# Unequal key halves for four maxima steps of a head pair, and a division that is split between its two multiplications

## The chip, the cores and the metric

The kernel runs on one core of one Trainium2 chip. Its time is the device time of one execution in microseconds, from the first to the last instruction with what lies around them. The engines are TensorE (PE in the profile; PEld is its unit that loads weights), VectorE (DVE), ScalarE (ACT), GpSimd (POOL) and SyncE (SP), which issues most of the DMA transfers.

## The reference

Two blocks follow each other. The first is attention in which a query sees only the keys of its own cluster; the second is a feed-forward block with the activation h * erf(softplus(h)).

```
q, k, v: (4, 8, 768, 64) float32; centroids: (8, 16, 64)
q_assign = argmax(q_n . c_n); k_assign = argmax(k_n . c_n)      # normalised, 16 clusters
mask = q_assign[..., :, None] == k_assign[..., None, :]
scores = where(mask, q @ k^T / sqrt(64), -1e9)
scores = scores - max(scores, axis=-1, keepdims=True)
attn = exp(scores);  attn = attn / (sum(attn) + 1e-9)
x = (attn @ v) as (3072, 512)
h = x @ w_in;  g = h * erf(softplus(h));  out = g @ w_out       # w_in (512, 2048), w_out (2048, 512)
```

## The kernel before, in words

The attention block takes the 32 heads in 16 pairs (p = 0 to 15); the heads of a pair, e = 0 and 1, lie on partitions 0 to 63 and 64 to 127, so the two heads' multiplications use different rows of TensorE's array and run side by side. Each pair has 12 units u: two halves of 384 queries (half), and for each six blocks of 128 keys (j). A period (function `period(p, i)`, i = 0 to 5) works on two units. Everything from the period on is written in the order in which the engines shall do it: the class `InOrder` keeps the program's order on TensorE, VectorE, ScalarE and GpSimd. DMAs on SP are outside of that order there.

**Maxima.** The shift of the softmax of pair p + 1 is made while pair p is worked on. `maxima_step(p, i)` takes 128 queries (block t) against one half of the 768 keys: a product of the queries' and keys' bf16 copies ("qv", "kv"; in the profile wide<-kv,qv), then the cluster mask as a product of one-hot rows ("qm", "km"; wide<-km,qm), both into the PSUM tile `wide`, of which there is one; then VectorE reduces the two heads' rows to their negated maxima, `nmx` (nmx<-wide). Each period does two such steps, the two key halves of one query block: `step_ahead(u)` at its beginning, whole, and `step_ahead(u + 1, True)`, whose three pieces are set between other work. That second step's mask product uses 32 rows of each head, and the scores' mask product the other 32. Because the tile is single, each step's first multiplication waits for the step before to be reduced. The steps of the coming pair begin in period i = 3 of the pair before it: periods 3 and 4 (the fourth and fifth of a pair) have its blocks t = 0 and 1, period 5 has t = 2.

**Units.** `products(u)` multiplies queries and keys in float32 (sc<-qT,kT, two passes each) into one of two PSUM buffers `sc`; `scores(u)` adds the mask and the shift (sc<-qm,km); `curve(u)` is the exponential on ScalarE; `accumulate` sums on GpSimd, and `attend` multiplies by v (turned<-pr,in_v), two units later. A period's order on TensorE is: first maxima step, products of both units, second step's product, scores of the first unit, second step's mask product, scores of the second unit, then (in i = 3 the similarities of pair p + 2 with the centroids) attend, and in i = 0 and 3 the sums for a division.

**Routing.** In i = 3, `choose(p + 2, ...)` finds the clusters on VectorE: a transpose (sims), the maxima of 16 similarities, which it writes into the buffer of the period's second unit (sc<-sims), and the comparison with them (hot<-sims,sc). Between these VectorE does one or two operations on a weight that is being prepared (`bounded`, `shifted`), in pairs 1 to 11.

**Division.** `divide(u)` runs after the last unit of a half, in i = 3 for the first half and in i = 0 for the second. TensorE sums, ScalarE makes the inverse inv, and the generator stops. In the next period it goes on after the first maxima step: VectorE makes `den` and two multiplications in place, one for each k; it stops, and goes on after the second step's maximum with the write of x (more_out<-den,turned) and four DMAs to `x_dram`:

```
        mask(0)()
        next(part[0], None)      # den and the multiplications
        ...
        products(u)
        products(u + 1)
        mask(1)()
        second = step_ahead(u + 1, True) if u > 0 else iter(())
        next(second, None)
        scores(u)
        next(second, None)
        mask(3)()
        next(second, None)       # the second step's maximum
        next(part[0], None)      # x
        scores(u + 1)
```

The feed-forward block that follows uses products of Strassen-Winograd form and isn't touched.

Of the kernel before, what the change touches and what calls it, by code (L numbers as in the profile page):

```python
# [14 lines left out]
ALU = mybir.AluOpType  # L15
ACT = mybir.ActivationFunctionType
AX = mybir.AxisListType
PSUM = bass.MemoryType.PSUM

P = 128  # L20
B, H, S, D = 4, 8, 768, 64
# [4 lines left out]
HW = S // 2  # L26
QW = HW // 2
TW = QW + 2
HJ = NJ // 2
HP = H // 2  # L30
NPAIR = B * HP
# [39 lines left out]
def kernel(  # L71
# [55 lines left out]

    lowest = [const.tile([P, HJ, P], BF16, name=f"lowest{i}") for i in range(2)]
    maxima = [const.tile([P, 2, NJ, 3], F32, name=f"nmx{i}") for i in range(2)]
# [7 lines left out]
    def part_of(i, lo, n):  # L137
        return more_out[:, i].rearrange("p f m -> p (f m)")[:, lo : lo + n]
# [3 lines left out]

    prs = [const.tile([P, 2, 2, TW], F32, name=f"pr{i}") for i in range(NPT)]

# [52 lines left out]
    for base, pattern, sign, op, fill in (  # L197
# [5 lines left out]
            out=first, in_=first, compare_op=op, fill=fill, base=base, pattern=pattern,  # L203
# [61 lines left out]
    for e in range(2):  # L265
        for n in range(2):
            r = e * D + n * Q
# [11 lines left out]
    cn = setup[:, D : 3 * D].rearrange("p (e d) -> p e d", e=2)  # L279
    spare = iter(range(TW, HW))  # L280

# [98 lines left out]
    def maxima_step(p, i, sm=wide, behind=False):  # L380

        st = pairs[p]
        nmx = maxima[p % 2]
        t, half = divmod(i, 2)

        def passes(a, b, start, rows):
            for e in range(2):
                r = slice(e * D + rows.start, e * D + rows.stop)
                te.matmul(
                    sm[:, e, 0:HW], lhsT=st[a][r, t * P : (t + 1) * P],  # L390
                    rhs=st[b][r, half * HW : (half + 1) * HW], start=start, stop=not start,
                )

        passes("qv", "kv", True, slice(0, D))
        if behind:
            yield
        passes("qm", "km", False, slice(Q, D) if behind else slice(0, D))
        if behind:
            yield
        ve.tensor_reduce(  # L400
            out=nmx[:, :, t, half], in_=sm[:, :, 0:HW], axis=AX.X, op=ALU.max, negate=True
        )
        if i in (NJ - 1, 2 * NJ - 1):
            h = i // NJ
            ve.tensor_reduce(
                out=lowest[h][:, :, ::D].rearrange("p t e -> p e t"),
                in_=nmx[:, :, h * HJ : (h + 1) * HJ], axis=AX.X, op=ALU.min,
            )
            turns.append((p, h))

    def turn(p, h, copies=(ae.copy, ae.copy)):

        st = pairs[p]
        pn = turned[h][:, 0:HW].rearrange("p (t n) -> p t n", t=HJ)
        for t in range(HJ):
            for e in range(2):
# [50 lines left out]
    def accumulate(u):  # L467

        p, half, j = units[u]
        st = pairs[p]  # L470
        pr = prs[u % NPT]
        if j == 1:
            st["acc", half] = part_of(1 + half, 0, 2 * HW).rearrange("p (g x) -> p g x", x=QW)
        if j > 0:
            acc = st["acc", half]
            so_far = quarters(prs[(u - 1) % NPT]) if j == 1 else acc
            ge.tensor_tensor(out=acc, in0=so_far, in1=quarters(pr), op=ALU.add)

    def attend(u):

        p, half, j = units[u]
        st = pairs[p]
        if j == 0:
            st["av", half] = turned[half][:, 0 : 2 * TW].rearrange("p (k n) -> p k n", k=2)
        for k in range(2):
            for g in range(4):
                te.matmul(
                    st["av", half][g * Q : (g + 1) * Q, k], lhsT=st["v"][:, j, g // 2, k * Q : (k + 1) * Q],
                    rhs=prs[u % NPT][:, g // 2, g % 2], start=(j == 0 and k == 0), stop=(j == NJ - 1 and k == 1),
                )  # L490

    def divide(u):

        p, half, _ = units[u]
        st = pairs[p]
        av = st["av", half]

        psum = turned[1 - half][:, 0:QW]
        for g in range(4):
            te.matmul(psum[g * Q : (g + 1) * Q], lhsT=minus, rhs=st["acc", half][:, g], start=True, stop=True)  # L500

        if u + 1 < len(units):
            inv = routep.tile([P, QW], F32, name="inv")
            den = routep.tile([P, QW], F32, name="den")
        else:
            inv, den = part_of(0, 4 * HW, QW), part_of(1, 0, QW)
        ae.activation(out=inv, in_=psum, func=ACT.Ln, bias=alleps, scale=-1.0)
        ae.activation(out=inv, in_=inv, func=ACT.Exp, scale=-1.0)
        yield
        ve.scalar_tensor_tensor(  # L510
            out=den, in0=psum, scalar=S * EPS, in1=inv, op0=ALU.subtract, op1=ALU.mult
        )
        for k in range(2):
            raw = av[:, k, 0:QW]
            ve.scalar_tensor_tensor(
                out=raw, in0=raw, scalar=av[:, k, QW : QW + 1], in1=inv, op0=ALU.add, op1=ALU.mult
            )
        yield
        x = part_of(0, (2 * p + half) % 4 * HW, HW).rearrange("p (k x) -> p k x", k=2)
        ve.scalar_tensor_tensor(  # L520
            out=x, in0=den.unsqueeze(1).to_broadcast([P, 2, QW]), scalar=2.0, in1=av[:, :, 0:QW],
            op0=ALU.add, op1=ALU.mult,
        )
        b, r = divmod(p, HP)
        for g in range(4):
            rows_of, at = r * P + g // 2 * D, b * S + half * HW + g % 2 * QW
            nc.sync.dma_start(
                out=x_dram[rows_of : rows_of + D, at : at + QW].rearrange("(k r) x -> r k x", k=2),
                in_=x[g * Q : (g + 1) * Q],
            )  # L530
        if half == 1:
            del pairs[p]
        yield
# [209 lines left out]
    def step_ahead(u, behind=False):  # L743
        p, i = divmod(u + NJ, 2 * NJ)
        steps = maxima_step(p, i, behind=behind) if p < NPAIR else iter(())
        if not behind:
            run(steps)
        return steps
# [7 lines left out]
    def period(p, i):  # L756
# [78 lines left out]
        if u > 0:  # L835
            if i == 1 and early(n1 - 1):
                summed(n1 - 1)
            elif i == 4 and early(n1):
                summed(n1)
            for w in (u - 2, u - 1):  # L840
                accumulate(w)
            if i % HJ == 1 and p in POOL_FORMS and forms:
                forms.pop(0)[1]()
            for w in (u - 2, u - 1):
                attend(w)
            if i % HJ == 0:
                part[0] = divide(u - 1)
                next(part[0])
# [13 lines left out]
    st = pairs[0]  # L862
    st["qT"], st["kT"] = rows[0]["q"], rows[0]["k"]
    ve.transpose(out=st["qT"], in_=st.pop("q").rearrange("p n t -> p (n t)"))
    for e in range(2):
        ve.tensor_copy(
            out=ccT[e * D : (e + 1) * D, :, e * C : (e + 1) * C],
            in_=pct[e * D : (e + 1) * D].rearrange("d (r e c) -> d r e c", e=2, c=C)[:, :, e],
# [7 lines left out]
    for r in (0, D):  # L876
        for half in range(2):
            for e in range(2):
                c = r + half * Q + e * C
                ve.tensor_copy(  # L880
                    out=pick[r : r + D, half, e * D : (e + 1) * D].rearrange("p (n c) -> p n c", n=2)[:, :, 1 : C + 1],
                    in_=first[r : r + D, c : c + C].unsqueeze(1).to_broadcast([D, 2, C]),
# [16 lines left out]
    for i in range(NJ):  # L899
        run(maxima_step(0, i, also if i % 2 else wide))  # L900
        if i == 1:
            masks(0, "q", 1, turned[1])()
        if i < NJ - 1:
            warm(2, turned[0], zeros)
# [20 lines left out]
    for w in (u - 2, u - 1):  # L925
        attend(w)
    last = divide(u - 1)
    attention.close()

# [100 lines left out]
```

## Time and profile before

| | us |
|---|---|
| median of 3 runs | 997.11 (996.61 to 997.18) |
| profiled execution, its own time | 997.0 |
| its span, first to last instruction | 995.3 |
| TensorE busy | 987.6 |
| VectorE busy | 700.5 |
| ScalarE busy | 488.0 |
| GpSimd busy | 350.3 |

Matmuls overlap each other in the array, so "busy" for TensorE says that something was under way, not how well it was used. The granted clock was 1.0 throughout. A line of a timeline gives start and length in us, engine, line (62 for all, since a helper issues them), operation, output<-inputs, shapes and how often; a bracket gives the idle time before it and what is held to have ended it. A line of busy time by stretch gives the stretch and its length, then the busy time of PE, PEld, DVE, ACT and POOL with the number of instructions, the granted clock, the DMA engines' busy share and GB/s. The attention block fills about the first 400 us, 24.6 a pair.

### The profile page before, as it was taken

What the parts mean: (1) busy time and instruction counts of PE and PEld (TensorE: products, weight loads), DVE (VectorE), ACT (ScalarE), POOL (GpSimd) and SP (SyncE); (2) the same over time, 40 slices, a digit from 0 to 9 for tenths busy, and PEclk for the clock granted to TensorE, in tenths of its full rate; (3) what the DMA queues carried; (4) which work ended last, traced back from release to release, by engine and by line L of the source; (5) the groups of instructions that cost most, each with busy time, mean ns of one, the idle gap of its engine ahead of it and who ended that gap; (6) DMA issues with size and microseconds to landing.
All of it is one profiled execution on the core that took longest, in us unless ns stands there. A gap on an engine that the chain in (4) does not pass through costs nothing.

```text
span 995.3 us, 20543 instructions
## 1 busy us (share of the span) xinstructions
PE 987.6 (99%) x8362; PEld 743.0 (75%) x8362; DVE 700.5 (70%) x1347; ACT 488.0 (49%) x659; POOL 350.3 (35%) x237
## 2 busy tenths in 40 slices
PE   8999999999999999999999999999999999999998
PEld 3555555555555555688888888888888888888887
DVE  8888888888888876779676554756475647655653
ACT  3777777777776665575432414150505050505050
POOL 1687878787878888662400000000000000000000
PEclk9999999999999999999999999999999999999999
DMA  9444444444444210331000100010001000000001
GB/s 223 78 110 108 107 110 111 110 113 113 87 94 110 51 35 19 102 106 65 1 12 32 42 1 22 22 43 1 22 22 43 1 21 22 1 1 22 22 1 42
DMA packets 147294, 55.88 MB, mean 56 GB/s; under 512 B 128640, under 2 KB 137088, under 8 KB 147200
## 3 DMA queue, kind: packets, MB, share of 16 engines
q1 hardware_dynamic: 144848, 54.29, 21.5%
q8 instruction: 65, 1.06, 0.4%
q10 hardware_dynamic: 2352, 0.30, 0.2%
q14 instruction: 29, 0.24, 0.1%
HBM read 41.98 MB, written 12.58 MB: 55 GB/s over the span
## 4 chain that ended last, share of the span: by engine, by line
PE 96%; DVE 1%; POOL 1%; DMA 1%; issue 0%; ACT 0%; SPq 0%; ACTq 0%; DVEq 0%; POOLq 0%
PE bank L62 43%; PE turned L62 31%; PE sc L62 16%; PE wide L62 6%; POOL more_out L62 1%; DVE nmx L62 1%; DMA g_more<-in_moe_w_out_dram 0%; DMA in_q<-in_q_dram 0%; DVE sims L62 0%; POOL x_more L62 0%; DVE kT L62 0%; DVE qT L62 0%; ACT pr L62 0%; ACT w_out L62 0%; DVE turned L62 0%
## 5 line engine op out<-in xcount | busy, mean ns | idle before, releaser
L62 POOL TENSOR_TENSOR more_out<-more_out,pr 128x768 f32<-128x768 f32 x128 | 217.0, 1695 | 19.2 <-ACT pr L62 10.5
L62 DVE TENSOR_REDUCE nmx<-wide 128x2 f32<-128x768 f32 x189 | 180.6, 955 | 58.9 <-PE wide L62 57.7
L62 ACT ACTIVATE pr<-sc 128x768 f32<-128x768 f32 x192 | 148.8, 811 | 95.6 <-PE wide L62 91.0
L62 PE MATMUL turned<-pr,in_v 128*32 128x194 f32 x3072 | 145.5, 330 | 0.0
L62 PEld LDWEIGHTS turned<-pr,in_v 128*32 128x32 f32 x3072 | 91.5, 109 | 51.2 <-issue 21.3
L62 DVE TENSOR_TENSOR g<-bank,g 128x256 f32<-128x256 f32 x222 | 89.5, 421 | 53.3 <-PE bank L62 46.4
L62 PE MATMUL bank<-x_own,w_in 128*128 128x256 f32 x424 | 104.7, 380 | 0.8 <-DVE g L62 0.8
L62 PE MATMUL bank<-w_out,g 128*128 128x256 f32 x448 | 103.1, 379 | 0.0
L62 PE MATMUL sc<-qT,kT 64*128 64x384 f32 x528 | 98.3, 484 | 0.0
L62 PEld LDWEIGHTS bank<-w_out,g 128*128 128x128 f32 x448 | 85.1, 190 | 11.6
L62 PEld LDWEIGHTS bank<-x_own,w_in 128*128 128x128 f32 x424 | 80.3, 190 | 12.6 <-DVE g L62 1.2
L62 DVE TENSOR_TENSOR osb<-bank,osb 128x256 f32<-128x256 f32 x87 | 35.4, 419 | 72.8 <-ACT osb L62 25.4
L62 ACT COPY g<-bank 128x256 f32<-128x256 f32 x28 | 10.4, 371 | 153.0 <-PE bank L62 148.5
L62 ACT ACT_TABLE_LOAD x48 | 61.6, 1283 | 45.7 <-DVE g L62 45.0
L62 PE MATMUL bank<-x_more,more_in 128*128 128x256 f32 x296 | 76.0, 379 | 0.0
L62 POOL TENSOR_TENSOR more_out<-pr,pr 128x768 f32<-128x768 f32 x32 | 60.0, 1875 | 28.4 <-ACT pr L62 28.4
L62 PEld LDWEIGHTS sc<-qT,kT 64*128 64x128 f32 x528 | 51.8, 187 | 19.8 <-ACT inv L62 2.3
L62 PE MATMUL wide<-kv,qv 64*128 64x384 bf16 x378 | 64.9, 328 | 1.1 <-ACT km L62 0.6
L62 PEld LDWEIGHTS <-qv 64*128 64x128 bf16 x384 | 26.9, 93 | 51.8 <-issue 35.7
L62 PE MATMUL bank<-more_out,g_more 128*128 128x256 f32 x272 | 64.3, 379 | 0.0
L62 DVE TENSOR_TENSOR g<-a_s,g 128x512 f32<-128x512 f32 x96 | 62.4, 688 | 1.4 <-ACT a_s L62 1.4
L62 PE MATMUL wide<-km,qm 64*128 64x384 bf16 (+1 forms) x378 | 62.5, 327 | 0.0
(170 smaller groups left out, 1667.4 us busy)
## 6 DMA issues: line engine op xcount, KB each, us to landing
x_own<-in_moe_w_in_dram SPq DMA_DIRECT2D x13, 512.0 KB, 4.2
in_v<-in_v_dram SPq DMA_DIRECT2D x32, 192.0 KB, 2.9
x_dram<-more_out SPq DMA_DIRECT2D x128, 48.0 KB, 1.9
x_own<-x_dram SPq DMA_DIRECT2D x6, 1024.0 KB, 5.0
out_dram<-osb SPq DMA_DIRECT2D x23, 256.0 KB, 2.0
in_k<-in_k_dram SPq DMA_DIRECT2D x59, 96.0 KB, 2.6
in_q<-in_q_dram SPq DMA_DIRECT2D x58, 96.0 KB, 2.6
g_more<-in_moe_w_out_dram SPq DMA_DIRECT2D x6, 512.0 KB, 3.3
```

Of the source, the lines that this page charges most:

```text
L62: ins = getattr(self.engine, name)(*args, **kw)
```

## The change

In all pairs but the first, the two maxima steps of query blocks t = 0 and t = 1 divide the 768 keys into 256 and 512 instead of 384 and 384. These are the steps of the fourth and fifth periods of the pair before. The number of multiplications and reductions is the same, only their widths differ.

In the division of the first half, the stop that stood after both multiplications now stands after the first: den and the first multiplication come behind the first maxima step, the second multiplication and the write of x behind the second step's maximum. The division of the second half stops where it did.

```diff
+FIRST_KEYS = {0: 256, 1: 256}
@@ maxima_step
         t, half = divmod(i, 2)
+        to = FIRST_KEYS.get(t, HW) if p else HW
+        keys = slice(to, S) if half else slice(0, to)
+        sm = sm[:, :, 0 : keys.stop - keys.start]
 
         def passes(a, b, start, rows):
             for e in range(2):
                 r = slice(e * D + rows.start, e * D + rows.stop)
                 te.matmul(
-                    sm[:, e, 0:HW], lhsT=st[a][r, t * P : (t + 1) * P],
-                    rhs=st[b][r, half * HW : (half + 1) * HW], start=start, stop=not start,
+                    sm[:, e], lhsT=st[a][r, t * P : (t + 1) * P], rhs=st[b][r, keys], start=start, stop=not start,
                 )
...
         ve.tensor_reduce(
-            out=nmx[:, :, t, half], in_=sm[:, :, 0:HW], axis=AX.X, op=ALU.max, negate=True
+            out=nmx[:, :, t, half], in_=sm, axis=AX.X, op=ALU.max, negate=True
         )
@@ divide
             ve.scalar_tensor_tensor(
                 out=raw, in0=raw, scalar=av[:, k, QW : QW + 1], in1=inv, op0=ALU.add, op1=ALU.mult
             )
-        yield
+            if k == half:
+                yield
```

## The prediction

> **What bounds the kernel now.** I read the page first (busy time, chain, costliest groups), then busy time by stretch for three neighbouring periods of two head pairs, then the timeline of those periods, engine by engine.
>
> ```profile
> span 995.3 us, 20543 instructions
> ...
> PE 987.6 (99%) x8362; PEld 743.0 (75%) x8362; DVE 700.5 (70%) x1347; ACT 488.0 (49%) x659; POOL 350.3 (35%) x237
> ...
> PE 96%; DVE 1%; POOL 1%; DMA 1%; issue 0%; ACT 0%; SPq 0%; ACTq 0%; DVEq 0%; POOLq 0%
> ...
> L62 DVE TENSOR_REDUCE nmx<-wide 128x2 f32<-128x768 f32 x189 | 180.6, 955 | 58.9 <-PE wide L62 57.7
> ```
>
> TensorE sets the time, and what delays it is paid in full. VectorE, 70% on average, is fuller where the change lies. Busy time by stretch of the fourth and fifth periods, first of pair 7, then of pair 12 (columns: length, then busy PE, PEld, DVE, ACT, POOL):
>
> ```profile
> 202.80:207.54 4.74, 4.74 (x73) 2.55 (x70) 3.89 (x7) 3.56 (x6) 3.14 (x2) 1.00 0.51 83
> 207.54:211.36 3.82, 3.82 (x57) 2.04 (x54) 3.75 (x8) 2.94 (x7) 3.28 (x3) 1.00 0.30 84
> 325.73:330.46 4.73, 4.73 (x72) 2.60 (x68) 3.73 (x6) 2.69 (x5) 3.50 (x3) 1.00 0.52 83
> 330.46:334.23 3.77, 3.77 (x56) 2.09 (x53) 3.61 (x7) 2.23 (x5) 2.74 (x3) 1.00 0.02 4
> ```
>
> In pair 7 VectorE is busy 3.75 of 3.82 us in the fifth period, which is 0.05 longer than pair 12's. Pairs 1 to 11 all look like pair 7 (3.81 to 3.82); 0, 12, 13 and 14 like pair 12 (3.76 to 3.77). The difference is two operations on a weight (bounded, shifted) that only pairs 1 to 11 have in the fourth period. VectorE's timeline of pair 7, from the fourth period's second maximum:
>
> ```profile
> 205.13 0.96 DVE L62 TENSOR_REDUCE nmx<-wide 128x2 f32<-128x768 f32 x1 [0.83 <-PE wide L62]
> 206.01 0.42 DVE L62 TENSOR_SCALAR w_in<-w_in 128x512 f32<-128x512 f32 x1
> 206.34 0.58 DVE L62 STREAM_TRANSPOSE sims<-turned 128x384 f32<-128x384 f32 x1
> 206.84 0.39 DVE L62 TENSOR_SCALAR w_in<-w_in 128x512 uint32<-128x512 uint32 x1
> 207.14 0.55 DVE L62 TENSOR_REDUCE sc<-sims 128x24 f32<-128x384 f32 x1
> 207.73 0.55 DVE L62 TENSOR_TENSOR hot<-sims,sc 128x384 bf16<-128x384 f32 x1
> 208.20 0.95 DVE L62 TENSOR_REDUCE nmx<-wide 128x2 f32<-128x768 f32 x1
> 209.07 0.35 DVE L62 SCALAR_TENSOR_TENSOR den<-turned,inv 128x192 f32<-128x192 f32 x1
> 209.33 0.89 DVE L62 SCALAR_TENSOR_TENSOR turned<-turned,inv 128x192 f32<-128x192 f32 x2
> 210.13 0.95 DVE L62 TENSOR_REDUCE nmx<-wide 128x2 f32<-128x768 f32 x1
> ```
>
> From 205.13 there is no idle bracket: a longer first entry pushes everything behind it. TensorE and its weight loads over the same stretch:
>
> ```profile
> 207.87 1.47 PE L62 MATMUL sc<-qT,kT 64*128 64x384 f32 x8
> 209.21 0.34 PE L62 MATMUL wide<-kv,qv 64*128 64x384 bf16 x2
> ```
>
> ```profile
> 208.40 0.33 PEld L62 LDWEIGHTS sc<-qT,kT 64*128 64x128 f32 x4 [0.33 <-ACT inv L62]
> ```
>
> The eight multiplications are the products of two key blocks. The second block's buffer held the routing maxima that the comparison "hot" reads until 208.28. Its weights are loaded at 208.40, 0.33 after the load unit fell idle; ScalarE is named, but the load follows the end of hot. In pair 12, where hot ends 0.41 after the period's start instead of 0.74, all eight loads run without a gap and the eight multiplications take 1.45. So in pairs 1 to 11 hot ends just in time: of the second block's two streams the first starts on time (208.52) and the second 0.02 late, 0.26 after hot's end.
>
> **The change, part by part.**
> *Fewer keys first.* A 384-key multiplication follows its predecessor by 0.162 us (207.71 to 207.87), so 128 keys are 0.054. Each period's first step has two stacks (its two heads run side by side), so it gives TensorE 2 x 0.054 = 0.108.
>
> *More keys second.* The centred product of the second step runs alone: +0.054. Its mask product shares the array with the first block's score products, which use other rows; the second block's scores follow 0.17 later on the rows of the first, ending 0.33 after the common start. A mask product of 512 keys takes 0.16 + 0.054 = 0.21 and ends inside that: 0. Its cover is the second block's scores; if they had to wait for it, +0.054. Net: -0.054 a period.
> On that cover: at 192.75 one score multiplication of the second block starts while the other waits for a mask gather on its own rows until 192.92, so rows advance separately, though no row has unequal widths. "TensorEngine Tiling (Array Packing)", section "Key Properties", in the Trainium skill, says more: tiles work independently, and only a change of tiling mode drains the array. By it the cost is 0 and the sum below stands; without it, the sum would be 1.0 us higher.
>
> *The maxima.* The 768-element reduction takes 955 ns, the routing maximum of 384 elements 551 (a group row): 1.052 ns an element. So 512 elements: 686 (-269), 1,024: 1,224 (+269). Bounds for the long one: 955, if width were free, and 955 x 4/3 = 1,273. I take the line, since its two points are the same operation.
>
> *Fourth into fifth period, pairs 1 to 11.* The second step's multiplications start 0.108 earlier and take 2 x 0.054 longer, so the long maximum starts at 205.13 as now and ends 0.269 later. The whole queue shifts: hot ends at 208.55. The second block's products, which TensorE would want at 208.52 - 0.054 - 0.108 = 208.36, get their second stream at 208.55 + 0.26 = 208.81. Two passes of 0.32 bring the fifth period's second step to 209.45 (209.21 now): +0.24. The fifth period's first maximum, queued behind hot, is 0.269 late and 0.269 shorter, ends at 209.15 as now, and no longer decides. Then +0.054 for 512 keys; the 0.01 by which today's mode change was longer than an undisturbed one (0.266 against 0.255) goes. **+0.283 a pair.** The three gains (0.108, 0.054 from the fourth period, and the wait of 0.05 of today) are inside that figure: all are spent waiting for hot.
>
> *Division.* Per pair VectorE does the same four operations; the second multiplication moves behind the fifth period's second maximum. From the fifth period's start at 0 (pairs 1 to 11): mask product at 2.22 (1.94 + 0.283), its maximum 0.445 later as in the fourth period plus 0.054 = 2.72, ending 3.94. The moved multiplication follows (entries overlap by 0.083): 3.86 to 4.29. The write of x needs its result; between two such dependent operations lies 0.035 today (209.75 to 209.79), so x runs 4.32 to 4.87. The sixth period's first maximum, ready at 4.10 + 0.54 = 4.64, starts at 4.78 and ends 5.74. TensorE's second step there waits for its tile: it can go 0.052 after that, 5.79, and wants to at 4.10 + 1.625 = 5.73: **+0.065.** Bounds: 0, if the overlaps are a little better; 0.10, if the dependent pair costs a further 0.035. Today VectorE idles 0.36 before that maximum; the move and the longer reduction use it up. The size counts from the second step alone, so it falls in all 15 pairs.
> Without the move the multiplication would stand before the long maximum, where den and two of them end by 209.9 and the maximum is ready only at 210.26: there it was hidden.
>
> *The other pairs.* 14 has no routing: -0.108 + 0.065 = -0.043. In 0, 12 and 13 the transpose sims waited for TensorE, not VectorE: it slips 3.47 - 3.30 = 0.17, hot ends at 0.58 instead of 0.41, the second stream may start at 0.84 and TensorE wants it at 0.824: +0.017. -0.108 + 0.017 + 0.065 = -0.026.
>
> *Costed at nothing.* x leaves 0.9 later, and so do its four DMAs on SP; the next loads behind them on SP are issued some 4 us after x (186.97, then 191.25). POOL's queue is not touched. The bank that the moved multiplication and x use is next written by the mask gather at 213.42 (pair 7), x ends at 212.4: cover 1.0 us before TensorE would wait. ScalarE has only idle time after TensorE here. Key loads and DMAs do not change.
>
> **Sum:** 11 x (0.283 + 0.065) = 3.83; 3 x -0.026 = -0.08; -0.04. +3.7 us on the profiled 997.0 = 1000.7; the median of the runs lies 0.1 above it: **1000.8 us** (+0.37%). A measurement here tells about 0.2% (2.0 us) from no change.
>
> **Rivals.**
> 1. *Hot's delay alone*: the sixth period's wait doesn't come (its margin is 0.065 of a chain of 5.8). 11 x 0.283 - 3 x 0.091 - 0.108 = +2.7: 999.8. For it: six overlaps go into that chain; against: it comes in each pair alike.
> 2. *The 512-key mask product holds the scores*: +0.054 in 15 fifth periods and in the 4 fourth periods that no hot swallows: +1.0, 1001.8. Against it: rows seen advancing separately.
> 3. *Not slower: hot doesn't release the second block's products*, and the weight load is late for ScalarE's sake, as the view prints. Then the fifth period's second step starts at 209.21 as now (its maximum ends as now): 11 x (0.054 + 0.065) - 0.12 = +1.2, 998.3, within 0.2%. In general the forecast leaves "slower" where hot is less than about 0.12 late, since 11 x (0.12 + 0.014 + 0.065) - 0.12 is 2.1. Against it: pairs 12 and 13 with an early hot and no gap.
> 4. *Faster: VectorE takes the longer maximum without delaying hot or the sixth period*: 15 x -0.108 and 11 x -0.05, -2.2: 994.9. For it: TensorE's own work falls. Against it: no idle bracket from 205.13 on.
> 5. *The change doesn't do what it says*: the first maxima cost 955 whatever their width; then the fifth period's second step waits longer, over 1002.
>
> **How the numbers follow.** Forecast 0.64, rival 1 0.12, rival 2 0.10, rival 3 0.08, rival 4 0.04, rival 5 0.02. Slower: 0.64 + 0.12 + 0.10 + 0.02 = 0.88; same 0.08; faster 0.04. The range takes in rivals 1 and 2 and the bounds of the long maximum (1,273 for 1,224: 11 x 0.05 = +0.5) and goes 0.5 below rival 1: 999.3 to 1002.1.
>
> **What the profile after would show.** Two new maxima groups, 128x512 near 686 and 128x1024 near 1,224 ns, 30 each; in pairs 1 to 11 a gap of TensorE of some 0.4 us between the two blocks' products of the fifth period, weight loads right behind hot, and that period some 0.28 + 0.05 longer (its start comes 0.054 earlier); a maximum in the sixth period that no longer waits for TensorE; fourth periods 0.054 shorter, pair 14's fifth too. I am wrong if hot ends no later than today or if no gap stands behind it.

## The result and the profile after

The changed kernel takes 999.43 us (median of 10 runs, 998.95 to 1000.02), the kernel before, run beside it, 997.04 (996.61 to 997.18). The ratio is 1.0025 with a 95% interval of 1.0017 to 1.0033: slower by 2.4 us, a quarter of a per cent. I had forecast slower, by 3.7 (1000.8, with a range of 999.3 to 1002.1).

First, the page of the changed kernel, and from its groups of VectorE, shapes kept apart, the three widths of the maxima:

```profile
span 997.3 us, 20543 instructions
...
PE 988.9 (99%) x8362; PEld 739.4 (74%) x8362; DVE 698.8 (70%) x1347; ACT 490.7 (49%) x659; POOL 350.4 (35%) x237
```

```profile
L63 DVE TENSOR_REDUCE nmx<-wide 128x2 f32<-128x768 f32 x129 | 123.2, 955 | 37.2 <-PE wide L63 36.7
L63 DVE TENSOR_REDUCE nmx<-wide 128x2 f32<-128x1024 f32 x30 | 36.8, 1226 | 24.2 <-PE wide L63 24.2
L63 DVE TENSOR_REDUCE nmx<-wide 128x2 f32<-128x512 f32 x30 | 20.5, 684 | 1.4 <-PE wide L63 1.3
```

The prices of the widths are as worked out from two rows of before (686 and 1,224 ns); the busy time of every engine is within 0.6% of what it was. What moved is visible only by stretch. The fourth and fifth periods of pair 7, then of pair 12:

```profile
203.89:208.83 4.94, 4.89 (x71) 2.39 (x69) 3.79 (x7) 3.81 (x6) 3.10 (x2) 1.00 0.50 80
208.83:212.68 3.85, 3.85 (x57) 1.98 (x54) 3.37 (x7) 2.92 (x7) 3.57 (x3) 1.00 0.35 119
328.07:332.75 4.68, 4.68 (x71) 2.46 (x70) 3.40 (x5) 2.68 (x5) 3.50 (x3) 1.00 0.52 84
332.75:336.46 3.71, 3.71 (x56) 1.97 (x52) 3.20 (x6) 2.22 (x5) 2.73 (x3) 1.00 0.02 4
```

Pair 12 gained 0.05 in each (4.73 and 3.77 before). Pair 7 lost 0.20 in the fourth (4.74) and 0.03 in the fifth (3.82), and its fourth period has a stretch in which TensorE has nothing under way (4.89 busy of 4.94). VectorE's timeline of pair 7 from the fourth period's second maximum on:

```profile
206.17 1.23 DVE L63 TENSOR_REDUCE nmx<-wide 128x2 f32<-128x1024 f32 x1 [1.15 <-PE wide L63]
207.31 0.42 DVE L63 TENSOR_SCALAR w_in<-w_in 128x512 f32<-128x512 f32 x1
207.64 0.58 DVE L63 STREAM_TRANSPOSE sims<-turned 128x384 f32<-128x384 f32 x1
208.14 0.39 DVE L63 TENSOR_SCALAR w_in<-w_in 128x512 uint32<-128x512 uint32 x1
208.45 0.55 DVE L63 TENSOR_REDUCE sc<-sims 128x24 f32<-128x384 f32 x1
209.03 0.55 DVE L63 TENSOR_TENSOR hot<-sims,sc 128x384 bf16<-128x384 f32 x1
209.50 0.69 DVE L63 TENSOR_REDUCE nmx<-wide 128x2 f32<-128x512 f32 x1
...
212.38 0.42 DVE L63 SCALAR_TENSOR_TENSOR turned<-turned,inv 128x192 f32<-128x192 f32 x1
212.83 0.55 DVE L63 SCALAR_TENSOR_TENSOR more_out<-den,turned 128x384 f32<-128x384 f32 x1
213.30 0.95 DVE L63 TENSOR_REDUCE nmx<-wide 128x2 f32<-128x768 f32 x1
```

As before, nothing idles between the fourth period's second maximum and the fifth's first; the one that leads this queue is now the long one. The last entry, the sixth period's first maximum, has lost its idle bracket (0.36 before). TensorE's weight loads show where it waits:

```profile
208.34 0.19 PEld L63 LDWEIGHTS turned<-more_out,minus 128*32 128x32 f32 x8 [0.40 <-issue]
208.83 0.10 PEld L63 LDWEIGHTS <-qv 64*128 64x128 bf16 x2 [0.30 <-issue]
208.84 0.10 PEld L63 LDWEIGHTS <-qm 64*128 64x128 bf16 x2
208.95 0.30 PEld L63 LDWEIGHTS sc<-qT,kT 64*128 64x128 f32 x4
209.70 0.33 PEld L63 LDWEIGHTS sc<-qT,kT 64*128 64x128 f32 x4 [0.45 <-ACT inv L63]
```

There are two places, not one. The second block's products are loaded 0.12 after hot ends (209.03 + 0.55), as I had expected. But ahead of that the division's sums (turned<-more_out,minus) wait 0.40, until 0.12 after the routing transpose ends (207.64 + 0.58 = 208.22). Before the change that load had no gap:

```profile
207.03 0.20 PEld L62 LDWEIGHTS turned<-more_out,minus 128*32 128x32 f32 x8
```

The code has the reason: the similarities that the transpose reads and the first half's sums lie in the same columns of the same PSUM bank (`turned[1]`), so the sums may not be written until the transpose has read. I had not listed that wait.

### The profile page after: what moved, and what is told of

Its sections match the earlier page's. It is cut to its first block, busy times and chain, and to the rows that moved or that the text cites. A ratio compares the mean times of both kernels' runs of the same rounds, so it can differ in the third digit from the quotient of the medians.

```text
span 997.3 us, 20543 instructions
## 1 busy us (share of the span) xinstructions
PE 988.9 (99%) x8362; PEld 739.4 (74%) x8362; DVE 698.8 (70%) x1347; ACT 490.7 (49%) x659; POOL 350.4 (35%) x237
## 4 chain that ended last, share of the span: by engine, by line
PE 96%; DVE 1%; POOL 1%; DMA 1%; issue 0%; ACT 0%; SPq 0%; DVEq 0%; ACTq 0%; POOLq 0%
PE bank L63 43%; PE turned L63 31%; PE sc L63 16%; PE wide L63 6%; POOL more_out L63 1%; DVE nmx L63 1%; DMA in_q<-in_q_dram 1%; DMA g_more<-in_moe_w_out_dram 0%; DVE kT L63 0%; DVE qT L63 0%; DVE sims L63 0%; POOL x_more L63 0%; ACT pr L63 0%; SPq L63 0%; ACT w_out L63 0%
## 5 line engine op out<-in xcount | busy, mean ns | idle before, releaser
L63 DVE TENSOR_REDUCE nmx<-wide 128x2 f32<-128x768 f32 (+2 forms) x189 | 180.5, 955 | 62.8 <-PE wide L63 62.2
L63 PE MATMUL wide<-kv,qv 64*128 64x384 bf16 (+2 forms) x378 | 65.3, 328 | 1.1 <-ACT km L63 0.6
L63 PE MATMUL wide<-km,qm 64*128 64x384 bf16 (+3 forms) x378 | 62.4, 327 | 0.0
L63 PEld LDWEIGHTS bank<-x_more,more_in 128*128 128x128 f32 x296 | 56.2, 190 | 7.6
```

What stands on the lines that cost most here:

```text
L63: ins = getattr(self.engine, name)(*args, **kw)
```

## The experiments

All times stand beside runs of the kernel before on the same chip. Because TensorE repeats a period to a few nanoseconds from pair to pair, the length of a period, from the start of its first maxima step to the next one's, tells more than the total: the table gives it in us, from the traces.

| kernel | pair 7: 4th | 5th | 6th | pair 12: 4th | 5th | 6th | time | before |
|---|---|---|---|---|---|---|---|---|
| before | 4.735 | 3.819 | 3.930 | 4.733 | 3.763 | 3.930 | 997.04 | |
| changed | 4.940 | 3.847 | 3.942 | 4.684 | 3.715 | 3.943 | 999.43 | 997.04 |
| keys only | 4.939 | 3.842 | 3.929 | 4.684 | 3.715 | 3.928 | 999.35 | 997.13 |
| division only | 4.735 | 3.817 | 3.928 | 4.734 | 3.763 | 3.928 | 997.22 | 997.13 |
| fourth period's keys only | 4.940 | 3.828 | 3.928 | 4.684 | 3.764 | 3.930 | 999.33 | 997.13 |
| fifth period's keys only | 4.733 | 3.837 | 3.943 | 4.734 | 3.714 | 3.941 | 997.31 | 997.13 |
| shifted behind hot | 4.940 | 3.849 | 3.943 | 4.685 | 3.715 | 3.945 | 999.66 | 997.20 |
| bounded behind the transpose | 4.684 | 4.225 | 3.949 | 4.682 | 3.714 | 3.943 | 1001.01 | 997.25 |
| weight operations left out | 4.684 | 3.714 | 3.946 | 4.683 | 3.713 | 3.946 | 995.48 | 997.25 |
| before, left out too | 4.735 | 3.764 | 3.928 | 4.734 | 3.764 | 3.929 | 996.76 | 997.25 |

### Each part alone

```diff
 # keys only: the division as before
-            if k == half:
-                yield
+        yield
 # fourth, or fifth, period's keys only
-FIRST_KEYS = {0: 256, 1: 256}
+FIRST_KEYS = {0: 256}      # or {1: 256}
```

> The keys are divided 256/512 as in the changed kernel; the division keeps both multiplications ahead of the stop, as before. My theory (the long maximum of the fourth period delays the routing transpose and comparison on VectorE, and TensorE waits for them): nearly all of the loss stays, 11 x 0.236 us in the fourth and fifth periods of pairs 1 to 11, and only the 0.015 us a pair of the sixth period go: 999.2 us. Rival (the moved multiplication is what costs): the time falls to that of before or below, 997.0 or less.

> Keys 384/384 as before; only the division's stop is moved. My theory: the maximum of the fifth period starts up to 0.23 us earlier, the moved multiplication and x end 0.1 us before VectorE is wanted in the sixth period, TensorE waits nowhere: 997.0 us. Rival (the moved multiplication costs): up to the whole loss, 999.4.

> Unequal keys in the fourth period alone (256/512 for the first query block), division in two parts. My theory: the start of the fifth period comes 0.206 us later in pairs 1 to 11, as in the changed kernel, and the fifth period takes some 0.02 longer; the other four pairs gain 0.05: 999.3 us. Rival (the fifth period's steps or the division cost): about 997.

> Unequal keys in the fifth period alone (256/512 for the second query block), division in two parts. My theory: nothing is late in the fourth period; the fifth is bounded by the comparison hot at 0.74 after its start, takes 3.83 us instead of 3.82 in pairs 1 to 11, plus 0.015 in the sixth; the others gain 0.04: 997.2 us. Rival (the loss is the fifth period's): 999 or more.

Measured, as ratios to the kernel before with their 95% intervals: keys only 1.0023 (1.0014 to 1.0031), division only 1.0002 (0.9993 to 1.0010), fourth period's keys 1.0023 (1.0014 to 1.0032), fifth's 1.0003 (0.9994 to 1.0012). Each time came within 0.25 us of what I had expected. So the loss belongs to the keys of the fourth period. The divided division costs 0.012 to 0.015 us in the sixth periods of the table, and only together with the long maximum of the fifth; left undivided, both multiplications are over just when that maximum can start (0.43 after its mask product with and without the division), and nothing is lost. The divided version without the long maximum costs nothing either.

### Which wait: the order on VectorE

```diff
 # shifted behind hot
-            if early(n1):
-                shifted(n1)
             for _ in range(2):
                 next(routing[0], None)
+            if early(n1):
+                shifted(n1)
 # bounded behind the transpose (in another kernel)
         elif i == 3 and early(n1):
-            bounded(n1)
             sign(n1)
...
             if early(n1):
+                bounded(n1)
                 shifted(n1)
```

> The changed kernel, with the weight operation shifted put behind the comparison hot on VectorE instead of between the routing transpose and the routing maxima. The transpose is as late as in the changed kernel, hot 0.30 us earlier. My theory (two waits, the division's sums behind the transpose and the second block's products behind hot): the first stays, so the fourth period of pairs 1 to 11 stays at 4.94 us; the second goes, so the fifth falls from 3.85 to 3.71; the sum is 11 x 0.119 - 4 x 0.086 = +1.0 against before: 998.0 us. Rival (hot alone, as I had predicted): the fourth period falls back to 4.73 or less too, and the time to 996 to 997.

> The changed kernel, with the weight operation bounded moved behind the routing transpose on VectorE, so that the transpose is 0.33 us earlier and the comparison hot as late as before the move. My theory (hot's end sets the sum, the transpose only decides how much of the same wait is taken at the division's sums): the fourth period of pairs 1 to 11 falls to 4.68 us, the fifth grows from 3.85 to 4.10, and the time stays: 999.4 us. Rival (the wait for the transpose is what costs): 11 x 0.25 less, 996.7.

Shifted behind hot: 1.0025 (1.0016 to 1.0035), not the 998.0 that I had expected; its timeline on VectorE says why:

```profile
207.99 0.57 DVE L63 STREAM_TRANSPOSE sims<-turned 128x384 f32<-128x384 f32 x1
208.68 0.56 DVE L63 TENSOR_REDUCE sc<-sims 128x24 f32<-128x384 f32 x1
209.27 0.55 DVE L63 TENSOR_TENSOR hot<-sims,sc 128x384 bf16<-128x384 f32 x1
209.75 0.42 DVE L63 TENSOR_SCALAR w_in<-w_in 128x512 uint32<-128x512 uint32 x1
210.08 0.69 DVE L63 TENSOR_REDUCE nmx<-wide 128x2 f32<-128x512 f32 x1
```

The routing maxima need the transpose's result and start 0.11 after its end, where an independent neighbour starts 0.08 before its predecessor's end. `shifted`, in between, had filled that gap: moving it brings hot forward by 0.10, not 0.30. And the fifth period's first maximum now stands behind `shifted` and ends late; TensorE waits for the tile `wide` instead (second step 1.644 after the period's start, 1.622 in the changed kernel). The wait changed its name and kept its length. The fourth period stayed at 4.94, as its wait is for the transpose.

Bounded behind the transpose: 1.0037 (1.0023 to 1.0051). The fourth period falls to 4.684, pair 12's in the changed kernel, which shows that the transpose held the sums. The fifth grows by more, for `shifted` now depends on its neighbour `bounded`, and hot ends 0.13 later than in the changed kernel (5.820 against 5.695 us from the fourth period's start). VectorE, then TensorE's weight loads, then TensorE, of this kernel:

```profile
209.04 0.84 DVE L63 TENSOR_SCALAR w_in<-w_in 128x512 f32<-128x512 f32 x2
209.80 0.55 DVE L63 TENSOR_REDUCE sc<-sims 128x24 f32<-128x384 f32 x1
210.38 0.55 DVE L63 TENSOR_TENSOR hot<-sims,sc 128x384 bf16<-128x384 f32 x1
```

```profile
211.05 0.33 PEld L63 LDWEIGHTS sc<-qT,kT 64*128 64x128 f32 x4 [0.83 <-ACT inv L63]
```

```profile
210.03 0.81 PE L63 MATMUL sc<-qT,kT 64*128 64x384 f32 x4
211.08 0.59 PE L63 MATMUL sc<-qT,kT 64*128 64x384 f32 x2 [0.24 <-DVE hot L63]
```

The whole wait stands in one place now, and is large enough that TensorE's own bracket names hot, where the weight loads name ScalarE. Fourth and fifth together: 8.909 here, 8.787 changed, 8.554 before. The time is 3.8 us above before, 1.4 more than the changed kernel's 2.4; by the table it should be 11 x 0.12 = 1.3. That hot's end sets the sum of the two periods here is shown; that the time would stay was wrong by the dependent pair's gap.

### The weight operations out of the way

```diff
 # left out, from the changed kernel and from the one before
         elif i == 3 and early(n1):
-            bounded(n1)
             sign(n1)
...
-            if early(n1):
-                shifted(n1)
 # weights early: moved to the third period (and both with the keys only, and in the kernel before)
             step_ahead(u)
+        if i == 2 and early(n1):
+            bounded(n1)
+            shifted(n1)
```

> The changed kernel without bounded and shifted for the eleven weight pieces that have them in the fourth period (these two operations on VectorE are left out, nothing else). My theory: all pairs behave like pair 12, 0.086 less than before in the fourth to sixth periods: 15 x -0.086 = -1.3, 995.7 us. Rival (the loss does not need the weight operations in the queue): 998 or more.

> The kernel before without the same two operations. My theory: pairs 1 to 11 lose the 0.053 us of their fifth period and nothing else: 996.5 us, some 0.7 above the changed kernel without them. Rival: as fast as that kernel.

Left out (such a kernel does not compute the reference; it serves to find the cause): 0.9982 (0.9973 to 0.9991) for the changed kernel, 0.9995 (0.9986 to 1.0004) for before. Every pair is then like pair 12, and the unequal keys are ahead by 1.3 us (995.48 against 996.76), close to 15 x 0.083 = 1.2 from the table (12.344 against 12.427 for the three periods of pair 7). I had put the lead at 0.7 to 0.8, since I had counted the 0.086 of pair 12 as the gain of pairs 1 to 11 too, which lose their 0.053 besides. So the gain on TensorE is real in all fifteen pairs; eleven of them give it back, and more, to VectorE's queue. Pair 7 of the changed kernel without the two operations, by stretch:

```profile
201.96:206.64 4.68, 4.68 (x71) 2.47 (x69) 3.40 (x5) 3.56 (x6) 3.13 (x2) 1.00 0.54 87
206.64:210.36 3.72, 3.72 (x57) 1.98 (x54) 3.20 (x6) 2.93 (x7) 3.17 (x3) 1.00 0.24 58
```

> The changed kernel, with both weight operations (bounded, shifted) moved from the fourth period to the third, between its two maxima, where VectorE has 0.96 us of idle time. My theory: pairs 1 to 11 then behave like pair 12 of the changed kernel, whose fourth to sixth periods take 0.086 less than before: 15 x -0.086 = -1.3, 995.7 us, faster than before. Rival (TensorE itself works longer with 256 and 512 keys, or the loss is the division's): no better than 997.

> The kernel before with the same two weight operations moved to the third period. My theory: pairs 1 to 11 lose the 0.053 us by which their fifth period is longer than pair 12's: 11 x -0.053 = -0.6, 996.5 us. So the unequal keys are worth some -0.7 once VectorE has room. Rival (the move of the weight operations alone makes the whole gain): as fast as the changed kernel with them moved.

> Unequal keys, weight operations in the third period, division undivided as before. My theory: both multiplications are done before the long maximum of the fifth period can start, and the sixth period's maximum is no longer late: 0.015 us a pair less than with the division in two parts, 15 x -0.101 = -1.5, 995.5 us. Rival (the split of the division is needed to keep the long maximum on time): above 995.7.

Measured 1010.69, 1012.33 and 1010.98 (before: 997.20): all three far slower, in a place that the move itself made. The fourth to sixth periods do what was expected (4.684 and 3.713 in pair 7 with the unequal keys, 4.734 and 3.763 without; the undivided division again saves the sixth period's wait, 3.928 against 3.947). But the third period takes 5.52 to 5.55 instead of 4.09 in pairs 1 to 11. From the first of these kernels, VectorE, GpSimd and TensorE:

```profile
207.45 2.70 DVE L63 TENSOR_SCALAR w_in<-w_in 128x512 f32<-128x512 f32 x2
210.07 0.95 DVE L63 TENSOR_REDUCE nmx<-wide 128x2 f32<-128x768 f32 x1
```

```profile
206.36 7.08 POOL L63 TENSOR_TENSOR more_out<-more_out,pr 128x768 f32<-128x768 f32 x4
```

```profile
211.29 0.34 PE L63 MATMUL turned<-identb,lowest 128*32 128x128 bf16 x6 [1.26 <-DVE lowest L63]
```

The same two operations that took 0.42 and 0.39 in the fourth period take 0.89 and 1.79 here, and the shift of the softmax waits for the queue behind them. The last section says what the traces show of the cause.

### Keys where there is room

```diff
-FIRST_KEYS = {0: 256, 1: 256}
+FIRST_KEYS = {4: 256}
+ROOMY_KEYS = {0: 256, 1: 256, 4: 256}
-        to = FIRST_KEYS.get(t, HW) if p else HW
+        to = (ROOMY_KEYS if p == 1 or p > 12 else FIRST_KEYS).get(t, HW) if p else HW
-            if k == half:
+            if k == 1 - half:
```

> 256 and 512 keys only where VectorE's queue has room: for the first two query blocks in the pairs whose fourth period has no weight operations (0, 12, 13, 14), and for the fifth query block of every pair but the first, whose steps lie in the second period; the first half's division is left undivided, the second half's is stopped between its multiplications. My theory (each period gains 0.054 us of TensorE where the longer maximum delays nothing): 15 x -0.054 for the second periods and 4 x -0.10 for the others, -1.2: 995.9 us, fast but less than what a measurement can tell; the second period takes 3.71 us instead of 3.764. Rival (no period gains, TensorE's multiplications are no shorter in sum): 997.1.

Measured 1002.14, 1.0047 (1.0034 to 1.0060). The second period does fall to 3.713, but the third grows from 4.09 to 4.52:

```profile
201.15 0.55 DVE L64 SCALAR_TENSOR_TENSOR more_out<-den,turned 128x384 f32<-128x384 f32 x1
```

```profile
201.76 0.32 PE L64 MATMUL turned<-hotT,pick 64*128 64x384 bf16 x1 [0.26 <-DVE more_out L64]
```

The mask gather at the third period's start writes into `turned[1]`, where the second half's quotient lies until the write of x has read it; with the division split and the long maximum between its parts, x comes 0.5 later (3.87 us after the second period's start against 3.37). It ends 0.71 after the third period's start instead of 0.15, and the gather starts at 0.76 instead of 0.34. For the first half I had looked up the bank's next writer and found 1.0 us of cover; for the second half I had not. Apart from the kernels with operations left out, none was faster than the one before.

## Why the prediction was right or wrong

**What bounds, and the sign: right.** The fourth period's long maximum leads an unbroken queue on VectorE, and TensorE pays for it in pairs 1 to 11. Pairs 0, 12, 13 and 14 gain.

**The prices of width: right.** 684 and 1,226 ns for 686 and 1,224; a period without waits is 0.050 shorter (forecast 0.054).

**The size of hot's delay: too large by 0.05; this is the first of the two terms that were mis-sized.** I let the long maximum start where it did before, because the mask product, 0.054 longer, would end 0.054 later. In pair 7 hot's end moved by 0.216, counted from the fourth period's start (5.479 to 5.695), not 0.269, since the maximum starts 0.05 earlier: between the start of the second step's mask product and its maximum lie 0.438 with 384 keys and 0.439 with 512 (means of pairs 1 to 11). In the fifth period it is 0.431, against 0.414 with 384 keys (the kernel with the fourth period's keys only). The wider product costs 0 to 0.017 there. So the fourth and fifth periods together cost 0.235 (mean of pairs 1 to 11), not 0.283.

**The sixth period: the mechanism right, the size 0.015 for 0.065**, for the same reason; this is the second term. The long maximum of the fifth starts 0.43 after its mask product, where I had 0.445 + 0.054 = 0.50, and that wait is the small rest of a long chain. The sixth period's first maximum ends 1.57 after the period's start instead of the 1.64 that I had worked out, so the second step starts on time (1.626), and only 0.015 is left, between its product and the scores behind it.

**Where TensorE waits: half missed.** My list of what is queued behind the long maximum named hot's reader but not the transpose's: "fourth periods 0.054 shorter" was wrong by 0.26 (+0.205), and the fifth period, forecast 0.33 longer, grew by 0.03. The sum survived, since a wait taken earlier at the sums is not taken again at hot, which ends the chain in either case. Nothing in my prediction provided for that: it was luck.

**The other pairs**: -0.081 to -0.087 instead of -0.026 and -0.043. 0.05 of that is the sixth period's; most of the rest of 0, 12 and 13 is that hot delays no product there (their fifth period is as short as pair 14's, which has no hot).

Sum: 11 x 0.25 - 4 x 0.085 = +2.4, as measured; the forecast's 3.7 less 15 x 0.05 (sixth) and 11 x 0.05 (hot) and some 0.05 is the same. The measured 999.43 lies only 0.1 above the lower end of my range, 999.3: both mis-sized terms erred the same way.

**Rivals.** The scores held by the 512-key mask product: refuted. TensorE's timeline before, then after, fourth period of pair 7:

```profile
204.69 0.34 PE L62 MATMUL sc<-qm,km 32*128 32x384 bf16 x2
204.69 0.33 PE L62 MATMUL wide<-km,qm 32*128 32x384 bf16 x2
204.86 0.32 PE L62 MATMUL sc<-qm,km 32*128 32x384 bf16 x2
```

```profile
205.72 0.34 PE L63 MATMUL sc<-qm,km 32*128 32x384 bf16 x2
205.73 0.39 PE L63 MATMUL wide<-km,qm 32*128 32x512 bf16 x2
205.90 0.32 PE L63 MATMUL sc<-qm,km 32*128 32x384 bf16 x2
```

The second block's scores start 0.17 after the wide product, as before, though its 512 columns take some 4 x 0.054 = 0.22 to stream by the prediction's price. This is what "TensorEngine Tiling (Array Packing)" of the Trainium skill, section "Key Properties", states of tiles; now a row with unequal widths shows it. Weights loaded late for ScalarE's sake: refuted, the loads start 0.11 to 0.12 after hot's end through every reordering (after 0.45 idle, then 0.83). Hot's delay alone, without the sixth period's wait: closer than I gave it, 999.8 to the measured 999.4, though the wait that it denies does come, at a quarter of its size. Faster, with the longer maximum delaying nothing: not so here, but with the two weight operations left out the unequal keys do gain 1.3. The first maxima at 955 whatever their width: refuted by the 684.

## What to carry to other kernels

A reduction is priced not by its own engine's load but by who reads behind it: follow each entry of the queue to the buffer that it frees, by bank and columns, before saying where the wait will be. On an engine that works in order, independent operations between dependent ones are free up to the gap they fill; taking them out saves less than they last, and putting two dependent ones together costs the gap. An idle stretch on one engine need not be room: beside a busy neighbour the same operation can last longer, more than four times as long for `shifted` here.

## What the runs showed of the hardware

- Two VectorE operations with a scalar, both sides in SBUF, were held up beside GpSimd. `bounded` and `shifted` (128x512) take 0.42 and 0.38 to 0.39 in the fourth period, where GpSimd idles, and 0.86 to 0.89 and 1.78 to 1.80 in the third, beside its additions (1.7 each); in all eleven pairs of the three kernels each ended 0.28 to 0.29 after a GpSimd addition did. The Trainium skill, "SBUF — State Buffer", section "SBUF: two separate sides", states that VectorE in a mode of two ports and GpSimd take a shared pair of ports as a lock for a whole instruction. The durations and end times agree with that; that the lock is the cause is argued, for no run here took it away.
- The first moment at which VectorE takes up the second step's result hardly follows the width of the multiplication that makes it: 0.438 and 0.439 from that product's start with 384 and 512 keys in the fourth period, and 0.414 and 0.431 in the fifth, where 128 keys are 0.054 of multiplication. The product starts together with score products of 384 columns. Why is open: nothing here separates the end of the product from the report of it.
- Dependent neighbours on VectorE: 0.11 from the end of the transpose to the start of the maxima that read it, 0.03 from the end of `bounded` to the start of `shifted` and from the maxima to hot; independent ones overlap by 0.08.
